# Windowed attention feeding a token and channel mixer on one core: more filler products in two places of the prologue, and a new order for three of the four hand-written period plans

## The chip, the cores and the metric

The kernel runs on one core of one Trainium2 chip. The metric is the device time of the whole program in microseconds (us). Lower is better. "Before" has a median of 307.49 us over 5 runs.

## What is computed

For each of 8 batches: 8 heads of attention over 576 positions with 64 dimensions, where a position sees the 32 positions on either side of it and 8 global positions (and the global positions see all and are seen by all). The attention output, laid out as 576 x 512, is the input x of a mixer block with four weights:

```
x = attention(q, k, v, global_idx)            # 576 x 512 per batch
u = x + (relu(x^T @ w_tok1) @ w_tok2)^T       # across tokens: 576 -> 256 -> 576
out = u + relu(u @ w_ch1) @ w_ch2             # across channels: 512 -> 1536 -> 512
```

Nearly all multiplications are in the last line.

## The kernel before, in words

**The work of a batch.** All products are in 16-bit floats with sums in PSUM. Positions are cut into 5 row tiles (four of 128, one of 64), heads into 4 pairs. The steps of one batch, with the letters that the plans use for them and their lines:

- T, Q, K (L434 to L454): T transposes one head pair of q and k on TensorE, Q and K copy the result from PSUM to the tiles qT and kT (VectorE unless told otherwise). R and r (L459, L470) do so for the last 64 positions. CQ and CK (L418) cast q and k to 16 bits ahead of T, on ScalarE. LP (L404) loads q and k for a whole batch. From batch 3 on another way is taken: Z (L393) loads q or k with a cast, issued by GpSimd's queue, into zq or zk, and Y (L399) transposes it into qT or kT with a DMA that SyncE's queue (SP) issues.
- S and X (L479, L500): the scores of one head pair in two halves, each a PSUM tile, and the exponential of a half on ScalarE into e_all. From batch 4 on, SS, XA and XB (L506, L529, L535) do two pairs at a time. M (L542) multiplies the band mask in on VectorE, with the columns of the global keys first (eg). VO (L409) makes a shifted copy of v on VectorE.
- GK, LX, LM (L578, L590, L597): scores of the global queries, exponential on ScalarE, mask on VectorE. OG and RF (L601, L612): the global positions' values on TensorE and their masking on VectorE. OG needs M of all four pairs.
- PV and NO (L717, L749): probabilities times values for one row tile on TensorE, division by the sum on VectorE. PV needs RF.
- A, RU, H, AD (L761 to L805): the two token products with a relu between them on ScalarE, and the sum u on VectorE.
- U (L835) transposes u into uT by DMA on SP's queue, two row tiles for each of U.0 and U.1, and U.2 the last rows. In period 0 TensorE does it instead (P and UT, L847 and L856).
- M4, M4l (L861, L872): the first channel product in 12 column blocks, 4 products of 128x512 each, with a relu on ScalarE; M4l are the last rows of two batches. All M4 of a batch need all of its uT. M5 (L886): the second channel product for one row tile in two parts of 6 products; after the second part VectorE adds u, and SP's queue sends the tile out.

**The order.** Nothing is scheduled by a tool: every engine runs its instructions in the order in which the program records them. After a prologue (L928 to L1075), which does the attention and token product of batch 0, there are 8 periods. Period b takes the dense units of batch b (M4, M4l, M5, in this order, one at each "D") and, between them, what `PLAN` says for other batches: a word that starts with n is for batch b+1, m for b+2, o for b+3, b for batch b itself. PLAN[0] and PLAN[1] serve periods 0 and 1. PLAN[2] serves periods 2, 4 and 6, PLAN[3] periods 3, 5 and 7 (L1085). A word is the step and its arguments; a last "v", "m", 0 or 1 names the PSUM place.

**PSUM.** There are four pools: two of one buffer for scores and others (0 and 1), one of one buffer (v), and psM with two buffers (m), which the M4 and M5 blocks use too. Two steps that use the same buffer wait for each other: the second score half of a pair waits for the exponential of the half that was in its buffer.

**The queues.** Loads with a cast (Z, LV, weights) are issued by GpSimd in program order; output and DMA transposes (Y, U) by SP in program order. A step behind a waiting one on such a queue waits with it.

**The fillers.** W(n) (L236) issues n products of the identity with itself, 128x512 each, whose result nobody reads. With `fresh` it takes a new psM buffer, otherwise one that was set aside. In the prologue there are W(2), W(5), W(3), W(3), W(1) and W(3, True).

The places that change in the prologue: L957, behind the first score half S_(0, 0, 0) and ahead of S_(0, 1, 0); and between OG0(3) (L1032) and RF0(3), where TensorE's next work is M1_0(1), the first token product of batch 0. OG0, RF0, PV0, NO0 and M1_0 (L620 to L685) are the forms by head pair that only batch 0 uses.

Of the kernel before, what the change touches and what calls it, by code (L numbers as in the profile page):

```python
# [25 lines left out]

PLAN = [
    """
    D D D nR.0 D nr nGL D nT.0.v nQ.0 nCK.2 D D nK.0 nCQ.2 D nT.1.v nK.1 nQ.1 nCQ.3 nCK.3 mLP D nS.0.0.0 mLV nS.0.1.1
    nX.0.1 nX.0.0 D nT.2.v nQ.2 nK.2 D nS.1.0.0 nX.1.0 nM.0 nS.1.1.1 nX.1.1 nT.3.v D nK.3 nM.1 nS.2.0.0 nS.2.1.1 nX.2.0  # L30
    nX.2.1 nQ.3 D nM.2 nVO nGK.v nLX nLM nS.3.0.0 nX.3.0 nS.3.1.1 nX.3.1 D nM.3 D nOG.v nRF nPV.0.v nPV.1.1 nNO.0 nNO.1
    D mCQ nPV.2.v nNO.2 nPV.3.1 D nNO.3 mCK mCQ.2 nA.0.0 mCQ.0 mCQ.3 nPV.4.1 nNO.4 mCK.0 mCK.1 mR.m mr nA.1.0 nA.2.0
    nA.3.0 nA.4.0 nRU mCK.3 mCK.2 D mGL D mCQ.1 nH.0.v nAD.0 nH.1.0 nAD.1 D nP.0 nUT.0 mT.0.m nP.1 mQ.0 mK.0 mT.1.m mK.1
    mS.0.0.0 nUT.1 mS.0.1.1 mX.0.0 mX.0.1 mT.2.m mQ.1 mQ.2 mK.2 mM.0
    """,
    """
    mZ.0.1 mZ.1.0 mZ.1.2 mZ.0.4 nT.3.v nS.1.0.0 nS.1.1.1 mZ.1.1 nX.1.0 mZ.1.3 nQ.3 D nX.1.1 nK.3 D mZ.0.3 mZ.0.0 mZ.1.4
    D nS.2.1.1 mZ.0.2 nX.2.1 nS.2.0.0 nX.2.0 nM.1 nVO D nGK.v nLX nM.2 nS.3.0.0 nX.3.0 nS.3.1.1 nLM nX.3.1 D nM.3 D
    nOG.0 nRF D D nPV.0.v.h nPV.1.1 nNO.0 mY.0.2 mY.0.3 bHL nPV.2.0 bAT bU.2 mY.0.1 nNO.1 D mY.1.2 nNO.2 mY.0.0 D D
    nA.0.1 nPV.3.v nNO.3 nPV.4.0 nNO.4 mY.1.1 D nA.1.1 nA.2.1 D nA.3.1 mY.1.4 nA.4.1 mY.1.0 mY.0.4 nRU D mLV mY.1.3 D  # L40
    mGL nH.0.0 nAD.0 D nU.0 nH.1.1 nAD.1 nU.1 D D bGC bGT.0 oZ.1.2 bGE mS.1.0.v mX.1.0 D mS.0.0.1 mS.0.1.0 oZ.0.2 oZ.1.0
    mX.0.0 oZ.1.1 oZ.0.4 oZ.0.1 oZ.0.3 oZ.0.0 mX.0.1 oZ.1.3 D mS.1.1.0 mX.1.1 mM.0 mS.2.0.1 mX.2.0 mS.2.1.v mM.1 mX.2.1
    D mS.3.1.1 mS.3.0.0 mX.3.0 oZ.1.4 mX.3.1 D mM.2 mVO mM.3 D D mOG.0 mGK.v mLX mLM mRF D
    """,
    """
    D nPV.0.v.h nNO.0 nPV.1.1 mY.0.0 nNO.1 nPV.2.0 nNO.2 mY.0.2 bAT mY.0.3 D D nA.0.1 mY.1.2 nA.1.1 mY.1.4 mY.0.4 D
    nA.2.1 mY.1.3 nPV.3.v mY.1.1 nPV.4.0 mY.0.1 mY.1.0 nNO.3 D D nA.3.1 nNO.4 nA.4.1 nRU D D mLV nH.0.0 D nAD.0 nU.0 mGL
    D D nH.1.0 nAD.1 oZ.0.1 oZ.0.0 D nU.1 oZ.0.2 D mSS.0 mXA.0 mXA.1 mXB.0 oZ.0.3 oZ.0.4 oZ.1.1 D mM.0 D oZ.1.4 mM.1
    oZ.1.0 D oZ.1.3 D oZ.1.2 mSS.1 mXA.2 mXA.3 mXB.1 mVO D mM.2 mM.3 D mGK.v mLX mOG.1 mRF mLM D
    """,  # L50
    """
    D bHL mY.1.0 nPV.1.1 nNO.1 nPV.2.0 nPV.0.v.h nNO.0 mY.0.0 mY.0.1 bAT nNO.2 mY.1.1 D mY.0.2 bU.2 D D nA.0.1 nPV.3.v
# [8 lines left out]
def kernel(  # L61
# [13 lines left out]
    B, H, S, D = q.shape  # L75
# [29 lines left out]
    def psm(shape, dtype=F32, name="m"):  # L105
        return psM.tile(shape, dtype, tag="m", name=name)
# [129 lines left out]
    def W(n, fresh=False):  # L236
        w = psm([P, 512], name="warm2") if fresh else warm
        for _ in range(n):
            nc.tensor.matmul(w.rearrange("p (a x) -> p a x", a=4), lhsT=ident, rhs=fill, start=True, stop=True)  # L239
# [230 lines left out]
    def TRE(b, tis=(0, 1), eng=nc.vector.tensor_copy):  # L470
        for ti in tis:
            v_ = st[b]["pr"][:, ti].rearrange("p i (n x) -> p n x i", n=NP)
            dst = qTs[b % 2][:, :, NT - 1, Q0 : Q0 + LAST] if ti == 0 else kTs[b % 2][:, :, WIN + 512 : WIN + S]
            eng(out=dst.rearrange("p n (x i) -> p n x i", i=4), in_=v_)
# [4 lines left out]
    def S_(b, p, part, at=None):  # L479
        qf = qTs[b % 2][:, p].rearrange("p t x -> p (t x)")  # L480
        kT = kTs[b % 2][:, p]
        ps = psx(at, [P, 2, 512], name=f"s{part}_{b}_{p}")
        a, z = ((0, 2 * QS), (2 * QS, ES))[part]
        if b == 0:
            for par in range(2):
                nc.tensor.matmul(ps[:, par, 0 : z - a], lhsT=ident, rhs=band[:, 0 : z - a], start=True, stop=False)
        js = ((0, 1, 2, 3, 4), (4, 5, 6, 7, 8, 9))[part]
        for j in js:
            i0 = max(qcol(j - 1), a)
            i1 = min(qcol(j) + HQ + Q0 * (j % 2 == 0), z)  # L490
            o = slice(HQ * (j % 2), HQ * (j % 2) + HQ)
            for par in range(2):
                r = slice(64 * par, 64 * par + 64)
                nc.tensor.matmul(  # L494
                    ps[o, par, i0 - a : i1 - a], lhsT=kT[r, HQ * j : HQ * j + HQ], rhs=qf[r, i0:i1],
                    start=b > 0, stop=b > 0 or j in js[-2:],
                )
        st[b]["s", p, part] = ps
# [121 lines left out]
    def OG0(p):  # L620
        s = st[0]
        if "rf" not in s:
            s["rf"] = mb.tile([P, NP, 2, VW], F16, tag="rf", name="rf_0")
        ps = psm([P, 2, VW], name=f"og0_{p}")
        s["og", p] = ps
        r = slice(32 * p, 32 * p + 32)
        for c in range(NT):
            nc.tensor.matmul(
                ps[r], lhsT=eg[:, c, 2 * p : 2 * p + 2, :], rhs=vsh[0][:, c, 2 * p : 2 * p + 2, :],
                start=(c == 0), stop=(c == NT - 1),  # L630
            )

    def RF0(p):
        s = st[0]
        r = slice(32 * p, 32 * p + 32)
        nc.vector.tensor_tensor(
            out=s["rf"][r, p], in0=s["og", p][r], in1=blk[r, 2 * p : 2 * p + 2].unsqueeze(2).to_broadcast([32, 2, VW]), op=ALU.mult
        )
# [23 lines left out]
    def NO0(p):  # L662
        pq = st[0]["pv", p][:, :, 0 : NT * VW].rearrange("p r (c x) -> p c r x", c=NT)
        rr = tiny.tile([P, NT, 2], F32, tag="rr0", name=f"rr0_{p}")
        nc.vector.reciprocal(out=rr, in_=pq[:, :, :, D])
        nc.vector.tensor_tensor(
            out=x16s[0][:, :, P * p : P * p + P].rearrange("p c (r x) -> p c r x", r=2), in0=pq[:, :, :, 0:D],
            in1=rr.unsqueeze(3).to_broadcast([P, NT, 2, D]), op=ALU.mult,
        )

    def M1_0(p):
        s = st[0]
        if "a1" not in s:
            s["a1"] = mb.tile([P, 2, DM], F16, tag="a1", bufs=1, name="a1_0")
            s["u16"] = mb.tile([P, 4, DM], F16, tag="u16", name="u16_0")
            s["ul"] = mb.tile([P, DM], F16, tag="ul", name="ul_0")
            s["uT"] = mb.tile([P, 4, 512], F16, tag="uT", name="uT_0")
        cols = slice(P * p, P * p + P)
        ps = psm([P, 2, P], name=f"a1p0_{p}")
        for tt in range(2):  # L680
            for ch in range(NT):
                w = w1[:, ch, P * tt : P * tt + P] if ch < NT - 1 else w1l[:, P * tt : P * tt + P]
                nc.tensor.matmul(ps[:, tt], lhsT=w, rhs=x16s[0][:, ch, cols], start=(ch == 0), stop=(ch == NT - 1))
        s["a1p", p] = ps
# [269 lines left out]
    S_(0, 0, 0)  # L954
    TRE(0, (0,), A)
    TRE(0, (1,), V)
    W(3)  # L957
    S_(0, 1, 0)
    SX(0, 0, 0)
    load_w1()  # L960
# [69 lines left out]
    PV0(0)  # L1030
    NO0(1)
    OG0(3)  # L1032
    RF0(3)
    M1_0(1)
    NO0(0)
# [86 lines left out]
```

## Time and profile before

| | us |
|---|---|
| median of 5 runs | 307.49 |
| lowest, highest | 306.23, 310.38 |
| the profiled execution | 310.13 |
| its span, from first to last instruction | 308.3 |

The profiled execution lies 2.64 us above the median, near the highest of the runs. Its granted TensorE clock is 1.00 throughout. TensorE is busy for 289.9 us of the span (94%), VectorE for 169.1, ScalarE for 135.5, GpSimd for 104.0. The 16 DMA engines moved 41.81 MB.

The stages of the span, cut where the first M4 of each batch starts:

| stage | from, to (us) | length | TensorE not busy |
|---|---|---|---|
| prologue | 0, 37.87 | 37.87 | 9.69 |
| period 0 | 37.87, 78.60 | 40.73 | 3.31 |
| period 1 | 78.60, 117.50 | 38.90 | 0.22 |
| period 2 | 117.50, 148.20 | 30.70 | 0.42 |
| period 3 | 148.20, 183.70 | 35.50 | 0.00 |
| period 4 | 183.70, 214.30 | 30.60 | 0.42 |
| period 5 | 214.30, 249.80 | 35.50 | 0.00 |
| period 6 | 249.80, 277.50 | 27.70 | 0.00 |
| period 7 | 277.50, 308.30 | 30.80 | 4.31 |

In rows of the timeline the columns are start, duration, engine (SPq is SyncE's queue), line, operation, tiles (written<-read), shape and count; in square brackets the idle time before the row and what ended it. A row's start is more certain than its end. In rows of waits they are the waiting engine and line, what ended the wait, the sum in us, the number of times and the longest.

### The profile page before, as it was taken

How to read it: one execution, taken by the hardware profiler on the slowest of the kernel's cores; microseconds unless marked ns; L12 is line 12 of the kernel's file. 1: busy time of each engine (PE TensorE's matmuls, PEld its weight loads, DVE VectorE, ACT ScalarE, POOL GpSimd, SP SyncE). 2: the span in 40 equal slices, each digit the busy share in tenths (PEclk: the TensorE clock that was granted, in tenths of full speed). 3: DMA queues.
4: the chain of work that ended last, by engine and by line, in shares of the span. 5: the costliest groups of instructions: out<-in, count | busy, mean ns of one | idle time of the engine just before them, and what ended most of it. 6: DMA issues, size and time to landing. Idle time of an engine off the chain costs nothing.

```text
span 308.3 us, 7871 instructions
## 1 busy us (share of the span) xinstructions
PE 289.9 (94%) x3310; PEld 157.6 (51%) x3310; DVE 169.1 (55%) x374; ACT 135.5 (44%) x225; POOL 104.0 (34%) x143
## 2 busy tenths in 40 slices
PE   4797899798999999999999999999999999999994
PEld 1356654455556445544556445444546455444643
DVE  7588557867973587238723756257613952321022
ACT  4570468533854153554345513634366415305500
POOL 6847657867002391057315720095000000000000
PEclk9999999999999999999999999999999999999999
DMA  6989999999906999979999998499954220231023
GB/s 190 218 152 195 297 206 133 289 196 175 112 3 100 100 178 216 119 108 146 208 147 128 121 214 134 85 138 198 187 79 80 102 70 2 51 119 53 0 83 89
DMA packets 138166, 41.81 MB, mean 136 GB/s; under 512 B 125779, under 2 KB 132371, under 8 KB 138131
## 3 DMA queue, kind: packets, MB, share of 16 engines
q0 software_dynamic: 85408, 18.75, 66.5%
q1 hardware_dynamic: 52720, 22.56, 38.5%
q8 instruction: 26, 0.43, 0.6%
q14 instruction: 10, 0.07, 0.1%
q10 hardware_dynamic: 2, 0.00, 0.0%
HBM read 36.04 MB, written 9.44 MB: 148 GB/s over the span
## 4 chain that ended last, share of the span: by engine, by line
PE 81%; DVE 8%; issue 5%; ACT 4%; DMA 1%; SPq 0%; DVEq 0%; ACTq 0%
PE b1p L867 26%; PE op L893 25%; PE a1p L769 5%; PE hp L792 4%; PE b1lp L880 3%; PE pv L726 3%; PE pv L735 3%; PE pT L438 2%; PE s L494 2%; PE warm L239 1%; DVE e_all L551 1%; DVE vod L411 1%; ACT e_all L504 1%; ACT e_all L537 1%; PE sa L522 1%
## 5 line engine op out<-in xcount | busy, mean ns | idle before, releaser
L870 ACT ACTIVATE b<-b1p 128x512 f16<-128x512 f32 x96 | 57.3, 600 | 82.3 <-PE b1p L867 82.2
L867 PE MATMUL b1p<-uT,wc 128*128 128x512 f16 x384 | 91.3, 379 | 0.0
L893 PE MATMUL op<-wc,b 128*128 128x512 f16 x372 | 85.1, 380 | 0.0
L867 PEld LDWEIGHTS <-wc 128*128 128x128 f16 x384 | 36.0, 98 | 41.4 <-issue 0.3
L893 PEld LDWEIGHTS <-b 128*128 128x128 f16 x372 | 34.7, 98 | 40.6
L897 DVE TENSOR_TENSOR osb<-u,op 128x512 f32<-128x512 f16 x31 | 21.2, 684 | 35.4 <-PE op L893 34.9
L395 POOL DMA_DIRECT2D zq<-in_q_dram x25 | 21.0, 853 | 54.7 <-DMA qT<-zq 52.5
L803 DVE TENSOR_TENSOR u<-x,hp 128x1024 f16<-128x1024 f16 x14 | 17.0, 1221 | 39.4 <-PE hp L792 39.4
L388 POOL DMA_DIRECT2D vsh<-in_v_dram x35 | 31.1, 895 | 10.5 <-DMA zq<-in_q_dram 3.2
L395 POOL DMA_DIRECT2D zk<-in_k_dram x25 | 21.1, 877 | 29.7 <-DMA kT<-zk 27.0
L504 ACT ACTIVATE e_all<-s 128x576 f16<-128x576 f32 (+1 forms) x32 | 21.8, 723 | 10.7 <-PE s L494 9.5
L551 DVE TENSOR_TENSOR e_all<-e_all,bandm 128x656 f16<-128x656 f16 x56 | 25.5, 497 | 1.0
L756 DVE TENSOR_TENSOR x<-pv,rr 128x512 f16<-128x512 f32 x35 | 24.2, 692 | 1.2
L531 ACT ACTIVATE e_all<-sa 128x864 f16<-128x864 f32 x16 | 13.6, 890 | 16.0 <-issue 13.8
L726 PE MATMUL pv<-rf,lf 128*64 128x264 f16 x140 | 18.2, 280 | 1.1 <-DVE rf L615 1.1
L735 PE MATMUL pv<-vsh,e_all 128*64 128x66 f16 x336 | 18.0, 194 | 0.0
L735 PEld LDWEIGHTS <-e_all 128*64 128x64 f16 x560 | 17.3, 111 | 0.0
L755 DVE RECIPROCAL rr<-pv 128x8 f32<-128x8 f32 x35 | 7.1, 203 | 17.9 <-PE pv L735 17.8
L769 PE MATMUL a1p<-x,w 128*128 128x512 f16 x56 | 15.4, 380 | 0.0
L792 PE MATMUL hp<-a,w 128*128 128x512 f16 x58 | 14.8, 379 | 0.0
L735 PE MATMUL pv<-vod,e_all 128*64 128x66 f16 x224 | 14.6, 194 | 0.0
L546 DVE TENSOR_TENSOR eg<-e_all,egm 128x80 f16<-128x80 f16 x28 | 5.5, 195 | 12.7 <-ACT e_all L537 10.9
(190 smaller groups left out, 347.5 us busy)
## 6 DMA issues: line engine op xcount, KB each, us to landing
out_dram<-osb SPq DMA_DIRECT2D x31, 256.0 KB
wc<-in_moe_w_ch_dram POOLq DMA_DIRECT2D x6, 512.0 KB
vsh<-in_v_dram POOLq DMA_DIRECT2D x21, 128.0 KB
zq<-in_q_dram POOLq DMA_DIRECT2D x20, 128.0 KB
zk<-in_k_dram POOLq DMA_DIRECT2D x20, 128.0 KB
lq<-in_q_dram POOLq DMA_DIRECT2D x2, 1024.0 KB
lk<-in_k_dram POOLq DMA_DIRECT2D x2, 1024.0 KB
vsh<-in_v_dram POOLq DMA_DIRECT2D x14, 96.0 KB
```

What stands on the lines that cost most here:

```text
L388: nc.gpsimd.dma_start(out=vsh[b % 2][r0:r1, c, :, 0:D], in_=v[b, :, j0 : j0 + (r1 - r0), :].rearrange("h p d -> p h d"),)
L395: nc.gpsimd.dma_start(out=(zq, zk)[ti][0:n, c], in_=(q, k)[ti][b, :, P * c : P * c + n, :].rearrange("h p d -> p h d"))
L504: nc.scalar.activation(out=e2[:, :, a:z], in_=ps[:, :, 0 : z - a], func=AF.Exp, scale=scale)
L551: nc.vector.tensor_mul(out=e2[:, par], in0=e2[:, par], in1=bm)
L726: nc.tensor.matmul(ps[r0 : r0 + 64, hf, 0 : NP * VW], lhsT=s["lf"][:, HQ * t : HQ * t + HQ], rhs=s["rf"][:, 2 * g : 2 * g + 2], start=True ...
L735: nc.tensor.matmul(ps[r0 : r0 + 64, hf, VW * hh : VW * hh + VW], lhsT=e_all[:, h, lo : lo + HQ], rhs=(vod if t % 2 else vsh)[b % 2][:, tau ...
L756: nc.vector.tensor_tensor(out=x16s[b % 2][r, tau, :].rearrange("p (f h x) -> p f h x", f=2, h=NP), in0=pq[r, :, :, 0:D], in1=rr[r].unsquee ...
L769: nc.tensor.matmul(ps[tt], lhsT=w, rhs=x16s[b % 2][:, ch, :], start=(ch == 0), stop=(ch == NT - 1))
L792: nc.tensor.matmul(ps[:, i, :], lhsT=w2[:, ch, P * tau : P * tau + P], rhs=s["a1"][:, ch, :], start=(ch == 0), stop=(ch == 1),)
L867: nc.tensor.matmul(ps, lhsT=wc1[:, cc, P * j : P * j + P], rhs=s["uT"][:, cc, :], start=(cc == 0), stop=(cc == 3))
L870: nc.scalar.activation(out=s["b1"][:, j, :], in_=ps, func=AF.Relu)
L893: nc.tensor.matmul(ps, lhsT=w, rhs=wc2[:, j, :], start=(j == 0), stop=(j == NJ - 1))
```

## The change

1. W(3) at L957 becomes W(5).
2. A W(4, True) is put in behind OG0(3), ahead of RF0(3) and M1_0(1).
3. PLAN[0], PLAN[1] and PLAN[2] are written in another order. PLAN[3] stays. The same steps are in them, with a few in another PSUM place. PLAN[2] is in force three times, in periods 2, 4 and 6.

The fillers, and the plans (old, then new; of PLAN[0] up to the token product, of the others the stretches that differ most):

```diff
@@ prologue
     TRE(0, (1,), V)
-    W(3)
+    W(5)
     S_(0, 1, 0)
...
     NO0(1)
     OG0(3)
+    W(4, True)
     RF0(3)
     M1_0(1)
@@ PLAN[0]
-    D D D nR.0 D nr nGL D nT.0.v nQ.0 nCK.2 D D nK.0 nCQ.2 D nT.1.v nK.1 nQ.1 nCQ.3 nCK.3 mLP D nS.0.0.0 mLV nS.0.1.1
-    nX.0.1 nX.0.0 D nT.2.v nQ.2 nK.2 D nS.1.0.0 nX.1.0 nM.0 nS.1.1.1 nX.1.1 nT.3.v D nK.3 nM.1 nS.2.0.0 nS.2.1.1 nX.2.0
-    nX.2.1 nQ.3 D nM.2 nVO nGK.v nLX nLM nS.3.0.0 nX.3.0 nS.3.1.1 nX.3.1 D nM.3 D nOG.v nRF nPV.0.v nPV.1.1 nNO.0 nNO.1
+    D D D nR.1 D nr nT.0.v D nCQ.2 D nGL nK.0 D nQ.0 D nS.0.0.0 nCK.2 nT.1.v nCQ.3 nS.0.1.1 nCK.3 mLP mLV nX.0.0 nK.1
+    nQ.1 nX.0.1 D D nT.2.v nQ.2 nK.2 nM.0 nS.1.0.0 nX.1.0 nS.1.1.1 D nX.1.1 nT.3.v nK.3 D nS.2.0.0 nS.2.1.1 nM.1 nX.2.0
+    D nQ.3 nX.2.1 nM.2 nVO nGK.v nLX nS.3.0.0 nX.3.0 nS.3.1.1 nLM nX.3.1 D nM.3 D nOG.0 nRF nPV.0.v nNO.0 nPV.1.1 nNO.1
...
-    nA.3.0 nA.4.0 nRU mCK.3 mCK.2 D mGL D mCQ.1 nH.0.v nAD.0 nH.1.0 nAD.1 D nP.0 nUT.0 mT.0.m nP.1 mQ.0 mK.0 mT.1.m mK.1
-    mS.0.0.0 nUT.1 mS.0.1.1 mX.0.0 mX.0.1 mT.2.m mQ.1 mQ.2 mK.2 mM.0
+    nA.3.0 nA.4.0 nRU D mCK.3 D nH.0.v nH.1.0 nAD.0 mCK.2 mCQ.1 nAD.1 D nP.0 mGL nUT.0 mT.0.m mT.1.m mQ.0 mK.0 mK.1 nP.1
+    mS.0.0.0 nUT.1 mX.0.0 mS.0.1.1 mX.0.1 mT.2.m mQ.1 mQ.2 mK.2 mM.0
@@ PLAN[1]
-    mZ.0.1 mZ.1.0 mZ.1.2 mZ.0.4 nT.3.v nS.1.0.0 nS.1.1.1 mZ.1.1 nX.1.0 mZ.1.3 nQ.3 D nX.1.1 nK.3 D mZ.0.3 mZ.0.0 mZ.1.4
-    D nS.2.1.1 mZ.0.2 nX.2.1 nS.2.0.0 nX.2.0 nM.1 nVO D nGK.v nLX nM.2 nS.3.0.0 nX.3.0 nS.3.1.1 nLM nX.3.1 D nM.3 D
+    mZ.1.0 nT.3.v nS.1.0.0 mZ.1.2 nX.1.0 mZ.0.1 mZ.0.4 nS.1.1.1 mZ.0.0 nX.1.1 D D nS.2.1.1 mZ.0.2 nX.2.1 nK.3 nS.2.0.0
+    nX.2.0 mZ.1.1 mZ.1.4 nM.1 mZ.1.3 nQ.3 D nVO D nGK.v mZ.0.3 nS.3.0.0 nX.3.0 nS.3.1.1 nM.2 nX.3.1 D nLX nM.3 nLM D
...
-    D mS.3.1.1 mS.3.0.0 mX.3.0 oZ.1.4 mX.3.1 D mM.2 mVO mM.3 D D mOG.0 mGK.v mLX mLM mRF D
+    mX.2.1 mS.3.1.1 mS.3.0.0 D mX.3.1 oZ.1.4 mVO mX.3.0 mM.2 mM.3 D D mOG.0 mGK.1 mLX mLM mRF D
@@ PLAN[2]
-    D nPV.0.v.h nNO.0 nPV.1.1 mY.0.0 nNO.1 nPV.2.0 nNO.2 mY.0.2 bAT mY.0.3 D D nA.0.1 mY.1.2 nA.1.1 mY.1.4 mY.0.4 D
-    nA.2.1 mY.1.3 nPV.3.v mY.1.1 nPV.4.0 mY.0.1 mY.1.0 nNO.3 D D nA.3.1 nNO.4 nA.4.1 nRU D D mLV nH.0.0 D nAD.0 nU.0 mGL
-    D D nH.1.0 nAD.1 oZ.0.1 oZ.0.0 D nU.1 oZ.0.2 D mSS.0 mXA.0 mXA.1 mXB.0 oZ.0.3 oZ.0.4 oZ.1.1 D mM.0 D oZ.1.4 mM.1
-    oZ.1.0 D oZ.1.3 D oZ.1.2 mSS.1 mXA.2 mXA.3 mXB.1 mVO D mM.2 mM.3 D mGK.v mLX mOG.1 mRF mLM D
+    mY.1.3 D nPV.1.1 nPV.0.v.h nNO.0 mY.0.0 nNO.1 nPV.2.0 mY.1.4 nNO.2 mY.0.2 mY.1.1 bAT mY.0.3 D D nA.0.1 nA.1.1 mY.0.4
+    D nA.2.1 nPV.3.v mY.0.1 nPV.4.0 mY.1.0 nNO.3 mY.1.2 D D nA.3.1 D nNO.4 nA.4.1 nRU mLV D D nH.0.0 mGL nAD.0 nU.0 D D
+    nH.1.v nAD.1 oZ.0.1 D D mSS.0 oZ.0.4 D D oZ.1.1 oZ.1.4 oZ.0.2 mXA.0 mXA.1 nU.1 oZ.0.0 mXB.0 oZ.0.3 mM.0 mM.1 oZ.1.0
+    oZ.1.3 oZ.1.2 D D mSS.1 mXA.2 mXA.3 mXB.1 mVO D mM.2 mM.3 D mGK.v mOG.1 mRF mLX mLM D
```

In the built program TensorE has 6 products more (3316 for 3310); the other engines have the same instructions in another order. On SP's queue the two transposes of U.1 stand, in periods 1, 2, 4 and 6, behind the batch's first output tile instead of ahead of it; most transposes of Y change places among themselves, and so do the loads of Z on GpSimd's queue.

## The prediction

> **What bounds the kernel now.** I read the page first, then TensorE's waits, then the timelines of the places that change. The page names TensorE as the bound, and its clock as fully granted, so only time in which TensorE waits can be won, and only what makes it wait can be lost.
>
> ```profile
> PE 289.9 (94%) x3310; PEld 157.6 (51%) x3310; DVE 169.1 (55%) x374; ACT 135.5 (44%) x225; POOL 104.0 (34%) x143
> ...
> PEclk9999999999999999999999999999999999999999
> ```
>
> By stage (the table above) TensorE idles 9.69 us in the prologue, 3.31 in period 0, 0.22 in period 1, 0.42 in each of periods 2 and 4, nothing in 3, 5 and 6. So new orders for periods 0, 1, 2, 4 and 6 fight over 3.31 + 0.22 + 0.84 = 4.4 us at most. The waits of the whole span, as TensorE's own list names them:
>
> ```profile
> PE og L606 <- DVE eg L546: 1.4, 3, 0.6
> ...
> PE pv L649 <- issue: 1.1, 1, 1.1
> PE pv L726 <- DVE rf L615: 1.1, 1, 1.1
> ...
> PE pu L854 <- DVE uT L859: 0.7, 1, 0.7
> PE s L494 <- ACT e_all L504: 0.6, 1, 0.6
> ```
>
> **Part 1: two fillers more at L957.** TensorE's timeline of the prologue:
>
> ```profile
> 12.81 1.46 PE L239 MATMUL warm<-ident 128*128 128x512 f16 x3
> 14.06 0.61 PE L486 MATMUL s<-band,ident 128*128 128x288 f16 x2
> 14.61 0.32 PE L494 MATMUL s<-qT,kT 64*64 64x80 f16 x10
> 14.86 0.82 PE L239 MATMUL warm<-ident 128*128 128x512 f16 x3
> 15.52 0.39 PE L438 MATMUL pT<-ident,qn 128*128 128x128 f16 x4
> ```
>
> Start to next start, the first three fillers take (14.06 - 12.81)/3 = 0.42 us each, the later three (15.52 - 14.86)/3 = 0.22: the array ran at half speed until about 14.3 us. Two more fillers cost 0.84 if both are slow, 0.43 if both are fast. The first would start at 14.06 (slow), the second at 14.48 (fast): 0.64. The two L486 products behind them would then be fast: 0.55 falls to about 0.34 (18.32 to 18.66 for the same shape), so the sum is 0.64 - 0.21 = +0.43. Nothing covers it: SX, T(0,2), its copies and the chain down to NO0(1) follow this row in TensorE's order. Possible cover comes later, at 31.1, where a product of PV0(2) waits 1.14 us for "issue" with no semaphore; if that ends at a fixed time, up to 1.14 us of delay vanishes in it. Bounds 0 and +0.84; I take +0.43.
>
> The Trainium skill ("TensorE: Matmul & The Clock Gate", "The HAM clock gate") says that the clock is halved by default and after an idle window of about 3.4 us, freed after as much sustained work, and that the window runs free of the program. By the rule, fillers might free the clock earlier in executions where the window falls badly, up to one window of half speed (some 1.7 us) saved. By the row, the clock was free at 14.3 with three fillers, and the two new ones start at 14.06, too late to bring that forward. I count +0.43 by the row and keep the rule's gain for a rival.
>
> **Part 2: W(4, True).**
>
> ```profile
> 27.08 0.46 PE L628 MATMUL og<-vsh,eg 128*32 128x132 f16 x5
> ...
> 28.44 0.38 PE L683 MATMUL a1p<-x,w 128*128 128x128 f16 x4 [0.89 <-DVE x L666]
> ```
>
> Four fast fillers are 0.88 us. Five products of 132 columns end their issue at about 27.36, so the fillers run until 28.24, and M1_0(1) can't start before 28.44, where VectorE's x lands. The row's idle time covers them: 0. They shift with part 1 as x does. The price without cover would be 0.88. The other risk is the buffer: if M1_0(1) had to take og0_3's, it would wait for RF0(3), whose VectorE row starts at 28.41 and takes 0.30: +0.27. In the built program it takes the fillers' own buffer and waits for the same VectorE step as before. As to the clock, the gap of 0.89 us is far below the rule's 3.4, and the products behind it are fast, so nothing is gained either. I take 0, bounds 0 and +0.27.
>
> **Part 3: period 0.** Here lies the money.
>
> ```profile
> 51.97 0.78 ACT L504 ACTIVATE e_all<-s 128x736 f16<-128x736 f32 x1 [0.86 <-PE b1p L867]
> ...
> 52.80 0.35 PE L494 MATMUL s<-qT,kT 64*64 64x80 f16 x12 [0.64 <-ACT e_all L504]
> ...
> 55.67 1.14 DVE L411 COPY vod<-vsh 64x2112 f16<-64x2112 f16 x1
> 56.84 0.96 DVE L412 COPY vod<-vsh 64x2112 f16<-64x2112 f16 x1
> ...
> 58.92 0.46 PE L606 MATMUL og<-vsh,eg 128*32 128x132 f16 x17 [0.60 <-DVE eg L546]
> ...
> 59.73 0.70 DVE L615 TENSOR_TENSOR rf<-og,blk 128x528 f16<-128x528 f32 x1
> ...
> 60.48 0.30 PE L726 MATMUL pv<-rf,lf 128*64 128x264 f16 x2 [1.10 <-DVE rf L615]
> ```
>
> S.2's second half waits for X.1.1, OG for M.3, PV for RF: 2.34 us. But they are one chain: from the end of X.1.1 (52.75) VectorE works without a pause through M.1, Q.3, M.2, VO, LM, an output sum and M.3 to RF's end at 60.43, 7.68 us. PV starts there whatever TensorE does. The new order keeps VectorE's sequence from M.1 to RF as it is, so PV moves by as much as M.1 does. The new order brings S.0 up by 1 to 2 M4 blocks and X.1.1 behind M4(10)'s relu. Adding up TensorE's rows (0.86 per M4, 0.44 per T, 0.09 at each change between full and partial tiles), T.2 starts at 48.7, S.1.1 ends at 49.65, M4(10) ends at 50.7, its relu runs 50.95 to 51.55, X.1.1 some 51.45 to 52.24. Masking follows at 52.3 instead of 52.78: about -0.45. The 0.86 of idle time ahead of X.1.1 is not in the order (TensorE's products were through at 50.3 by their rows), so it may be this execution's own; without it the old order would lose less, and the new one gain nothing. Bounds -1.2 and +0.3; -0.45. The period's end (P, T, Q, K, 74 to 78.6) hangs on VectorE's copies, in the same order as before: 0, though T.1 now fills a gap of 0.69.
>
> **Part 4: period 1.** The rows show S.3 held to 83.84 by X.2.0, 0.21 beyond its place, and OG by M.3 for 0.15 net. In the new order two M4 stand between S.2 and S.3, so X.2.0 (some 82.3 to 82.95) is done before S.3 (83.5), and M.3 before OG: -0.36 to -0.46 by the sums; -0.4, bounds -0.5 and +0.3.
>
> **Part 5: periods 2, 4, 6.** The number of changes between full and partial tiles (0.09 us each) is the same in both programs, and OG's wait (M.3 behind XB.1, 0.42) keeps its place. What moves is U.1. SP's queue in period 2:
>
> ```profile
> 134.40 5.18 SPq L842 DMA_TRANSPOSE uT<-u  x4
> 139.67 9.81 SPq L898 DMA_DIRECT2D out_dram<-osb  x4
> ```
>
> The four transposes of uT were issued from 134.40 to 139.58 and landed, by their semaphores, at 137.87, 141.75, 144.42 and 145.56; M4(0) of batch 3 starts at 148.23, so there were 2.67 us to spare (period 4: 210.37 against 214.29, 3.92). Now U.1 is queued behind the first output tile, whose VectorE sum ends at 139.13: it goes out at about 139.7 and 141.0, 2.7 later. If its own latency of 7.3 stays, it lands at 148.3: period 2 waits up to 0.3, period 4 none, and period 6 has no loads beside it. "DMA: Bandwidth & Descriptors", "Issuing engines are not separate DMA queues", speaks against the change: all queues share the 16 engines, so U.1 now shares them with that output and with Z and V loads that GpSimd issues from 134.77 to 149. By the rule, another 1 us for the 256 KB output at the 195 GB/s that the stretch 142 to 150 shows (1.3): 1.3 + 0.3 in period 2 and nothing in 4. By the row it is the same queue with the same sum of work, whose fifth transfer landed at 147.21: 0. Bounds 0 and +2; +0.3.
>
> **The sum.** +0.43 + 0 - 0.45 - 0.4 + 0.3 = -0.12 us. On the profiled 310.13 that is 310.0; the median stands 2.64 below it, and I take the difference over: 307.4.
>
> **The rivals.** (a) Slower: uT comes late. With 2.67 spare in period 2 and 3.92 in period 4, landing decides once it is over 148.2 and 214.3; at 4 us later than before it costs 1.3 + 0.1, at 5.5 later 2.8 + 1.6 and 1 in period 6: between +1.4 and +5, 308.9 to 312. For: a queue at its fullest in exactly these stretches. Against: SP's queue carries no more than before. (b) Faster: the clock or period 0 gives more than the profiled execution tells. Half of one slow window in the prologue (0.85) or part 3 at its bound (1.2), with part 4 and no cost of part 1 and 5: -1.6 to -2, some 305.5. For: runs spread from 306.23 to 310.38, so some stage varies. Against: PV can't pass VectorE. (c) The fillers are the whole effect: both slow, the plans neutral: +0.84 + 0.27 = +1.1, 308.6. For: each is on TensorE's chain; against: the 1.14 us wait at 31.1 behind them.
>
> **How the numbers follow.** That gains and losses cancel within 1 us: 0.57, at 307.4. (a) 0.18, (b) 0.12, (c) 0.13. One per cent is 3.07 us, about what a measurement of this kernel can tell from no change; only the far parts of (a) and (b) pass it: slower 0.14, faster 0.06, within 0.80. The range reaches to the far side of (b), -0.4 of part 4 on top of -1.7 (305.4), and up to the bounds of parts 1, 2 and 5 together, +0.84 + 0.27 + 2 (310.6).
>
> **What would show it.** Right: five L239 products ahead of the second L486 row and everything behind later by about 0.4 until 31; M1_0(1) still released by x; PV of period 0 still released by RF, some 0.45 earlier than its stage's start would give; no wait ahead of OG in period 1; M4(0) of batches 3, 5 and 7 without a gap. Wrong: a gap ahead of those M4(0); L867 or L438 rows at 0.42 per 512 columns behind 15 us in one kernel alone; M1_0(1) waiting for RF0(3).

## The result and the profile after

| | before | changed |
|---|---|---|
| median (us) | 309.09 of 79 runs | 310.98 of 42 runs |
| lowest, highest | 305.30, 314.35 | 308.28, 314.69 |
| profiled execution, its span | 310.13, 308.3 | 312.9, 311.1 |

The ratio changed to before is 1.0085, with a 95% interval of 1.0066 to 1.0103: 2.0 to 3.2 us slower. Ratios here leave out executions more than 1.5% above their kernel's fastest, which also hides part of what a steadier clock wins, so where the fillers are the subject I give medians and counts over all executions. By the medians the loss is 1.9 us. The forecast was 307.4, in a range up to 310.6. Of the miss of 3.6 us, 1.6 is the base, whose median rose from 307.49 to 309.09 with more runs; the other 2.0 is the change, forecast at -0.1.

The page of the changed kernel says that TensorE is still the bound, but on the chain that ended last DMA has grown from 1% to 9%, and SP's queue from 0% to 5%. The chain before:

```profile
PE 81%; DVE 8%; issue 5%; ACT 4%; DMA 1%; SPq 0%; DVEq 0%; ACTq 0%
```

The page of the changed kernel, with its chain as the last line:

```profile
PE 291.6 (94%) x3316; PEld 157.7 (51%) x3316; DVE 168.2 (54%) x374; ACT 135.1 (43%) x225; POOL 103.7 (33%) x143
...
PEclk9799999999999999999999999999999999999999
DMA  6989999999909999399999997599943220141023
...
PE 75%; DMA 9%; DVE 5%; SPq 5%; ACT 3%; issue 1%; DVEq 0%
```

TensorE's list of waits (engine, line, what ended the wait, sum, times, longest) has a new first row. In the kernel before uT was in no row for L867.

```profile
PE b1p L867 <- DMA uT<-u: 2.9, 2, 1.7
...
PE og L606 <- DVE eg L546: 1.2, 3, 0.4
PE pv L726 <- DVE rf L615: 1.1, 1, 1.1
PE s L494 <- ACT e_all L504: 0.9, 1, 0.9
...
PE sa L522 <- DMA kT<-zk: 0.4, 1, 0.4
...
PE a1p L683 <- DVE x L666: 0.2, 1, 0.2
```

TensorE's timeline shows the two places: the first M4 of batch 3 and of batch 5, at the ends of periods 2 and 4.

```profile
149.59 1.04 PE L867 MATMUL b1p<-uT,wc 128*128 128x512 f16 x4 [1.68 <-DMA uT<-u]
...
217.06 1.04 PE L867 MATMUL b1p<-uT,wc 128*128 128x512 f16 x4 [1.22 <-DMA uT<-u]
```

Stage by stage (cut at the first M4 of each batch), changed minus before: prologue -0.93, period 0 +0.37, period 1 -0.56, period 2 +2.48, period 3 0, period 4 +1.40, periods 5 to 7 0. The sum is the 2.8 us between the spans. The first two vary by more than this from one execution to the next and period 1 by up to 0.35; the others repeat within 0.1 us unless something waits. For the kernel before this takes the starts of M4 from the rows: that of batch 1 is at 79.13, not at 78.60 as in the table of stages, so that period 0 takes 41.26 and period 1 38.38.

SP's queue in period 2 (start, duration of the issues, count) shows what happened to U.1.

```profile
133.56 2.51 SPq L842 DMA_TRANSPOSE uT<-u  x2
138.68 0.35 SPq L898 DMA_DIRECT2D out_dram<-osb  x1
139.08 3.50 SPq L842 DMA_TRANSPOSE uT<-u  x2
142.68 6.32 SPq L898 DMA_DIRECT2D out_dram<-osb  x3
```

U.1 goes out behind the first output tile, and its two issues take 3.50 us where U.0's take 2.51. By the completion events in the trace the two land at 148.15 and 149.55: 9.1 and 8.3 us after their issues. M4(0) starts at 149.59, with the last of them.

In period 4 U.1 moves further. The queue before, then in the changed kernel:

```profile
199.31 5.24 SPq L842 DMA_TRANSPOSE uT<-u  x4
205.22 10.32 SPq L898 DMA_DIRECT2D out_dram<-osb  x4
```

```profile
206.60 0.35 SPq L898 DMA_DIRECT2D out_dram<-osb  x1
207.01 3.55 SPq L842 DMA_TRANSPOSE uT<-u  x2
```

Counted from the period's start, U.1's last issue goes from 19.6 to 24.3 us.

### The profile page after: what moved, and what is told of

It reads as the page before. It is cut to its first block, busy times and chain, and to the rows that moved or that the text cites. A ratio compares the mean times of both kernels' runs of the same rounds, so it can differ in the third digit from the quotient of the medians.

```text
span 311.1 us, 7884 instructions
## 1 busy us (share of the span) xinstructions
PE 291.6 (94%) x3316; PEld 157.7 (51%) x3316; DVE 168.2 (54%) x374; ACT 135.1 (43%) x225; POOL 103.7 (33%) x143
## 4 chain that ended last, share of the span: by engine, by line
PE 75%; DMA 9%; DVE 5%; SPq 5%; ACT 3%; issue 1%; DVEq 0%
PE b1p L867 24%; PE op L893 23%; DMA uT<-u 5%; PE a1p L769 5%; PE hp L792 3%; PE b1lp L880 3%; PE pv L726 3%; PE pv L735 3%; SPq L402 2%; DMA lkr<-in_k_dram 2%; PE s L494 1%; SPq L842 1%; PE warm L239 1%; DMA kT<-zk 1%; PE pT L438 1%
## 5 line engine op out<-in xcount | busy, mean ns | idle before, releaser
L867 PE MATMUL b1p<-uT,wc 128*128 128x512 f16 x384 | 91.7, 379 | 3.0 <-DMA uT<-u 2.9
L867 PEld LDWEIGHTS <-wc 128*128 128x128 f16 x384 | 35.9, 98 | 45.4 <-DMA uT<-u 3.9
L388 POOL DMA_DIRECT2D vsh<-in_v_dram x35 | 30.7, 897 | 5.9 <-DMA lk<-in_k_dram 2.1
L504 ACT ACTIVATE e_all<-s 128x576 f16<-128x576 f32 (+1 forms) x32 | 21.5, 720 | 10.6 <-PE s L494 10.2
L531 ACT ACTIVATE e_all<-sa 128x864 f16<-128x864 f32 x16 | 13.6, 890 | 16.6 <-issue 13.8
L769 PE MATMUL a1p<-x,w 128*128 128x512 f16 x56 | 15.4, 380 | 0.0
L735 PE MATMUL pv<-vod,e_all 128*64 128x66 f16 x224 | 14.7, 194 | 0.0
L792 PE MATMUL hp<-a,w 128*128 128x512 f16 x58 | 14.6, 379 | 0.0
```

Source lines behind the costliest of these rows:

```text
L388: nc.gpsimd.dma_start(out=vsh[b % 2][r0:r1, c, :, 0:D], in_=v[b, :, j0 : j0 + (r1 - r0), :].rearrange("h p d -> p h d"),)
L504: nc.scalar.activation(out=e2[:, :, a:z], in_=ps[:, :, 0 : z - a], func=AF.Exp, scale=scale)
L735: nc.tensor.matmul(ps[r0 : r0 + 64, hf, VW * hh : VW * hh + VW], lhsT=e_all[:, h, lo : lo + HQ], rhs=(vod if t % 2 else vsh)[b % 2][:, tau ...
L769: nc.tensor.matmul(ps[tt], lhsT=w, rhs=x16s[b % 2][:, ch, :], start=(ch == 0), stop=(ch == NT - 1))
L792: nc.tensor.matmul(ps[:, i, :], lhsT=w2[:, ch, P * tau : P * tau + P], rhs=s["a1"][:, ch, :], start=(ch == 0), stop=(ch == 1),)
L867: nc.tensor.matmul(ps, lhsT=wc1[:, cc, P * j : P * j + P], rhs=s["uT"][:, cc, :], start=(cc == 0), stop=(cc == 3))
```

## The experiments

Theory A: the late U.1 of PLAN[2] (periods 2 and 4) is the whole loss. Theories B and C of the first four runs: the new order of loads and Y transposes, or the fillers and the clock. Each "over" or "under" is against the kernel before, run on the same chip.

**1. U.1 late, alone.**

```diff
-    ... D nU.1 oZ.0.2 D mSS.0 ... oZ.1.1 D mM.0 D oZ.1.4
+    ... D oZ.0.2 D mSS.0 ... oZ.1.1 D mM.0 nU.1 D oZ.1.4
```

> The kernel before, with nothing changed but the place of U.1 in PLAN[2]: behind M5(0,1), so that its two transposes stand behind the first output tile on SP's queue. Theory A (the place of U.1 in the queue is what costs): M4(0) of batch 3 waits 1 to 2 us for uT and that of batch 5 about 1 us, so the time is 2 to 3.5 us over the kernel before (ratio 1.007 to 1.011). Theory B (the new order of Z, Y and V loads crowds the transposes, U.1's place alone is harmless because the queue carries the same sum): 0 to +0.3 us, no wait ahead of M4(0). Theory C (fillers and clock): 0.

Ratio 1.0047 (1.0020 to 1.0075): 1.45 us over. Less than A asked, more than B and C. In the profile uT lands 0.27 us ahead of need in period 2, and period 4 is 0.43 longer; the rest of the 1.45 this one profile doesn't show.

**2. The changed kernel with U.1 early.**

```diff
-    nH.1.v nAD.1 oZ.0.1 D D mSS.0 ... mXA.0 mXA.1 nU.1 oZ.0.0
+    nH.1.v nAD.1 nU.1 oZ.0.1 D D mSS.0 ... mXA.0 mXA.1 oZ.0.0
```

> The changed kernel with U.1 of PLAN[2] moved back to right behind AD.1, ahead of the first output tile; all else as changed. Theory A: no wait ahead of M4(0) of batches 3 and 5; what remains is the gain of the prologue and of period 1, so 0 to 1.5 us under the kernel before (ratio 0.995 to 1.000). Theory B: uT still comes late, +2 to +3 us (1.007 to 1.010). Theory C: +1 us or more, without a wait ahead of M4(0).

Ratio 0.9972 (0.9942 to 1.0002), no wait ahead of any M4(0), periods 2 and 4 at 30.72 us as before. One word's place takes back 3.5 us (1.0085 less 0.9972, of 309). C falls, and B alone too, since all the new loads are still there.

**3. The whole new PLAN[2] alone** (its text is in the diff above).

> The kernel before with the whole new PLAN[2] and nothing else of the change. Theory A: as with U.1 alone moved, 2 to 3.5 us over the kernel before, and about the full loss of the change plus 0.5 to 1, since what it wins elsewhere is not in it. Theory B: also +2 to +3.5; it differs from A only by what U.1 alone gives. Theory C: within 0.3 us of the kernel before.

Ratio 1.0100 (1.0064 to 1.0136): 3.1 us over. Between this and run 1 stands something else in PLAN[2] that hurts only when U.1 is late. The profile has periods 2 and 4 longer by 1.88 and 1.30.

**4. The fillers alone** (both edits).

> The kernel before with the two edits of fillers alone (W(5) for W(3), and the new W(4, True)). Theory A: between -1 and +0.5 us: the two cold fillers cost up to 0.84, and the 1.14 us in which a product of PV0(2) waits for no semaphore, together with the gap ahead of M1_0(1), takes it back, or the stall is gone as in the profile of the changed kernel. Theory C (fillers and clock make the loss): +1.5 to +3 us.

Ratio 1.0001 (0.9976 to 1.0027); medians of all executions 308.11 against 308.73. This is A; the loss that C asked for isn't there.

**5. PLAN[0] alone.**

> The kernel before with the new PLAN[0] alone. Theory A (the VectorE chain of period 0 starts 0.45 us earlier, as predicted): 0.3 to 0.6 us under the kernel before. Theory B (the exponential X.1.1 is late by about a microsecond wherever it stands, and the new order puts more behind it): PV of period 0 starts 23 us or more after the period's start, where the kernel before shows 22.6, and the time is 0.3 to 1.2 us over the kernel before.

Ratio 1.0032 (1.0002 to 1.0063), 1.0 us over, but the medians of all executions are 307.82 and 307.31 with wide spread, and its profile has PV 21.6 us after the period's start: neither theory's picture. The gain of A isn't there; more is said below.

**6. PLAN[1] alone.**

> The kernel before with the new PLAN[1] alone. Theory A (S.3 and OG no longer wait in period 1, as predicted): period 1 takes 37.8 to 38.0 us instead of 38.4, the time is 0.3 to 0.6 us under the kernel before. Theory B (the period's new order of Y and Z, or U.1 of period 1 behind the first output tile, gives it back at the start of period 2): a wait ahead of M4(0) of period 2 and a time within 0.3 us of the kernel before or over it.

Period 1 takes 37.75 us in the profile (38.37 to 38.67 in all nine profiled kernels with the old PLAN[1]), and M4(0) of period 2 has no wait. The ratio, 0.9997 (0.9963 to 1.0031), can't resolve 0.5 us in its 14 runs: A by the profile, not by the time.

**7. New PLAN[2] with U.1 late, but with later loads.**

```diff
-    D nA.2.1 nPV.3.v mY.0.1 nPV.4.0 mY.1.0 nNO.3 mY.1.2 D D nA.3.1
+    D nA.2.1 nPV.3.v nPV.4.0 mY.1.0 nNO.3 mY.1.2 mY.0.1 D D nA.3.1
```

> The kernel before with the new PLAN[2], U.1 behind the first output tile, and one word more moved: Y.0.1 goes last of the batch's Y, so that the first Z load, which must wait for it, and with it the row of Z and V loads on GpSimd's queue starts about 2.6 us later than in the new PLAN[2]. Theory A (the early Z and V loads are what makes a late U.1 land so late): the loss falls from the 3.1 us of the new PLAN[2] to that of U.1 alone or under it, 0 to +1.5 us over the kernel before; U.1's last transpose lands 6 to 7 us after its issue. Theory B (the loads don't matter; the place on SP's queue alone costs, and the two earlier runs differ by chance): +2 to +3 us, latency still 8 us or more.

Ratio 1.0016 (0.9983 to 1.0049): of the 3.1 us most is gone, as A said. But only period 2 lost its wait, and there 1.2 of the 1.9 us by which uT lands earlier than in run 3 are an earlier issue; from issue to landing it still took 7.3. Period 4 is 1.13 us longer than before and its last transpose took 8.4 us to land, which is B's latency.

**8. U.1 late as in run 1, with earlier loads.**

```diff
-    D nA.2.1 mY.1.3 nPV.3.v mY.1.1 nPV.4.0 mY.0.1 mY.1.0
+    D nA.2.1 mY.0.1 nPV.3.v mY.1.3 nPV.4.0 mY.1.1 mY.1.0
```

> The kernel before with U.1 late as in the first experiment and, beside it, only the three transposes Y.0.1, Y.1.3 and Y.1.1 in another order, so that the first Z load finds its place free two transposes (2.6 us) earlier. Theory A (late U.1 and early loads together make the loss): 2 to 3.5 us over the kernel before, M4(0) of batch 3 waits 1 to 2.5 us, the last uT lands 8 us or more after its issue. Theory B (U.1's place alone): as in the first experiment, 0.5 to 1.5 us over, latency under 7 us.

Ratio 1.0202 (1.0147 to 1.0256), from 6 executions: 6.2 us over, more than either theory. TensorE's waits show a second victim that I hadn't thought of, the last transpose of K, for which SS.0 waits:

```profile
PE sa L522 <- DMA kT<-zk: 2.8, 2, 2.2
PE b1p L867 <- DMA uT<-u: 2.1, 2, 1.4
```

So here the transposes of Y that are still on their way land later, and through SS.0 they hold up the output tile and U.1 behind it: U.1's last issue comes 3.2 and 1.0 us later than in run 1, and it lands 7.6 us after it in both periods, not the 8 or more of A. That the early Z loads are the cause is argued, since the order of the Y transposes changed with them. This run mixes two waits and proves less than it was meant to.

**9 to 12. What is in flight beside U.1.** The changed kernel, each time with fewer bytes and the same instructions. `h` heads of 8 for Z (and in the same way for V), `w` columns of 512 for the output tile. The other heads of batches 5 to 7 are not loaded and the other columns not written, so these kernels only test the transfers:

```diff
+        h = H if b < 5 else 1
-            out=(zq, zk)[ti][0:n, c], in_=(q, k)[ti][b, :, P * c : ...
+            out=(zq, zk)[ti][0:n, c, 0:h], in_=(q, k)[ti][b, 0:h, P * c : ...
...
+                w = DM if tau or b not in (2, 4) else 64
-                nc.sync.dma_start(out=out[b, P * tau : P * tau + P, :], in_=osb)
+                nc.sync.dma_start(out=out[b, P * tau : P * tau + P, 0:w], in_=osb[:, 0:w])
```

Z cut:

> The changed kernel, but the Z loads of batches 5 to 7 (those issued in periods 2 to 4) move one head of eight: the rest of q and k of these batches isn't loaded, so that the attention of these batches is computed on stale data. Same instructions on every engine. Theory A (what is in flight beside U.1 delays it, and Z is most of it): U.1 lands within 6 us of its issue, no wait or under 0.3 us ahead of M4(0) of batches 3 and 5, the time is 0 to 1.5 us under the kernel before. Theory B (U.1's later issue alone): still 2 to 3 us over. Theory C (the output tile ahead of it on the queue): still 2 to 3 us over.

V cut:

> The changed kernel, but the V loads of batches 5 to 7 move one head of eight (the other seven keep the values of an earlier batch). Theory A with Z as the load that matters: 1 to 3 us over the kernel before, a little less than the changed kernel. Theory A with V as the load that matters (V's packets are in flight when U.1 lands): 0 to 1.5 us under the kernel before, no wait ahead of M4(0). Theories B and C: 2 to 3 us over.

Output tile cut:

> The changed kernel, but the first output tile of batches 2 and 4, the transfer ahead of U.1 on SP's queue, writes 64 columns of 512 (the rest of these two tiles is left unwritten). Theory C (U.1 waits for the 256 KB ahead of it): U.1 lands 1.3 us or more earlier, the time is at most 1 us over the kernel before. Theories A and B: 2 to 3 us over, U.1 lands as late as in the changed kernel within 0.5 us.

Z and V cut:

> The changed kernel with both the Z and the V loads of batches 5 to 7 cut to one head of eight (stale data in their place). Theory A: U.1 lands 3 to 5 us after its issue, no wait ahead of M4(0), 0.3 to 1.7 us under the kernel before. Theory B: 2 to 3 us over. Theory C: 1.5 to 3 us over.

Ratios: Z cut 1.0009 (0.9978 to 1.0039), V cut 1.0025 (0.9992 to 1.0057), output tile cut 1.0053 (1.0002 to 1.0104), both loads cut 0.9975 (0.9940 to 1.0011). Against the changed kernel's 1.0085 (1.0066 to 1.0103) each cut of a load takes something back, and both loads together take all of it; the output tile's cut isn't clear of it by the time. The profiles say how. Times after the start of period 2 / period 4, from SP's and GpSimd's issues and the completion events; M4(0) is due at 30.72:

| kernel | first Z load | last U.1 issued | last uT landed | from issue to landing | period longer by |
|---|---|---|---|---|---|
| before | 17.3 / 16.2 | 20.8 / 19.6 | 28.1 / 26.8 | 7.3 / 7.2 | 0 / 0 |
| 1, U.1 late | 17.0 / 16.7 | 23.6 / 23.7 | 30.5 / 31.1 | 6.8 / 7.4 | 0 / 0.43 |
| 2, changed, U.1 early | 15.4 / 14.8 | 20.2 / 19.8 | 28.1 / 28.1 | 7.9 / 8.4 | 0 / 0 |
| 3, new PLAN[2] | 16.2 / 14.9 | 24.6 / 24.3 | 32.5 / 32.0 | 7.9 / 7.6 | 1.88 / 1.30 |
| changed | 16.3 / 14.7 | 24.8 / 24.3 | 33.2 / 32.1 | 8.3 / 7.8 | 2.48 / 1.40 |
| 7, loads late | 18.4 / 18.1 | 23.4 / 23.4 | 30.7 / 31.8 | 7.3 / 8.4 | 0 / 1.13 |
| 8, loads early | 14.6 / 13.5 | 26.9 / 24.6 | 34.5 / 32.3 | 7.6 / 7.6 | 3.79 / 1.60 |
| 9, Z cut | 16.6 / 14.8 | 23.8 / 23.4 | 29.5 / 30.3 | 5.7 / 6.9 | 0.43 / 0 |
| 10, V cut | 16.2 / 15.1 | 24.1 / 24.0 | 32.0 / 30.7 | 7.9 / 6.6 | 1.37 / 0 |
| 11, output tile cut | 15.9 / 14.8 | 23.8 / 24.3 | 30.8 / 31.6 | 7.0 / 7.3 | 0.15 / 0.90 |
| 12, Z and V cut | 16.8 / 14.8 | 23.9 / 23.3 | 26.8 / 25.8 | 2.9 / 2.5 | 0.58 / 0 |

Wherever the last uT lands after 30.7, the period is longer by about the difference. The 0.43 and 0.58 of runs 9 and 12 come with SS.0's wait for the last Y, which the new order has beside (0.21 and 0.37 of idle time there, 0.42 in the changed kernel; the rest no row names). The output tile's cut brings the landing 2.3 us forward in period 2, as C asked, and 0.5 in period 4, as A asked. Of the 2.3, 1.0 is U.1's earlier issue, in an execution without SS.0's wait.

With the loads cut U.1 lands 2.9 and 2.5 us after its last issue; in the kernel before it took 7.3 and 7.2. Period 6, where no loads run, shows the same without any cut: there the changed kernel's U.1 stands behind the same output tile,

```profile
273.27 0.35 SPq L898 DMA_DIRECT2D out_dram<-osb  x1
273.67 2.53 SPq L842 DMA_TRANSPOSE uT<-u  x2
```

and lands 2.5 us after its last issue, as in the kernel before, where it stands ahead of the tile. The stretch from the first output tile's issue to the landing, in the changed kernel and in run 12 (columns: length; busy time of PE, PEld, DVE, ACT, POOL; clock; DMA share; GB/s):

```profile
138.60:149.60 11.00, 8.90 (x110) 4.10 (x108) 9.05 (x20) 3.30 (x6) 6.92 (x8) 1.00 2.07 165
```

```profile
136.30:141.00 4.70, 4.70 (x64) 2.31 (x63) 4.15 (x10) 1.18 (x3) 2.61 (x5) 1.00 0.94 181
```

The packets' own time adds up to 2.07 times what 16 engines have with the loads, and to 0.94 times with the loads cut: U.1's packets are in flight among many others.

**13. W(4, True) alone.**

> The kernel before with the new W(4, True) behind OG0(3) alone. Theory A (in part of the executions the clock is halved in a stretch that begins in the idle time ahead of M1_0(1), and these four fillers prevent it): the share of executions with a mean granted clock under 0.99 falls from about 0.5 to under 0.2, and the time is 0.5 to 1.5 us under the kernel before. Theory B (these fillers change nothing, as predicted): share as before, time within 0.3 us of it.

Medians of all executions 306.33 against 307.31, and A's count: a mean clock under 0.99 in 1 of 22, against 35 of 75 before on the same chip. The ratio, 1.0010 (0.9985 to 1.0036), shows none of this, for the reason given with the result. Over all runs of this study the count is 16 of 218 in the kernels with W(4, True), 59 of 125 in the others, 121 of 251 in the kernel before. Under 0.985, as low as the profiles below, it is 0 of 218 and 65 of 251.

**14. W(5) alone.**

> The kernel before with W(5) for W(3) alone. Theory A (the other fillers keep the clock; these two only cost): the share of executions with a mean clock under 0.99 stays at about 0.5, the time is 0.3 to 0.8 us over the kernel before. Theory B (these two keep the clock): the share falls under 0.2, and the time is 0 to 1 us under the kernel before.

10 of 22 under 0.99, ratio 1.0034 (1.0003 to 1.0066), medians 307.86 and 307.31: they don't keep the clock, and they cost, A.

**15. W(4, True) and the new PLAN[1].**

> The kernel before with only the two parts of the change that seem to gain: W(4, True) and the new PLAN[1]. Theory A (they add up): 1.3 to 2 us under the median of the kernel before over all its executions, share of executions with a clock under 0.99 below 0.15, and 4 to 5 us under the changed kernel. Theory B (one of them is chance): 0.3 to 1 us under.

Medians 306.97 against 308.09, 1.1 us under: between the theories, no more than W(4, True) alone gave. 0 of 22 under 0.99. Ratio 0.9981 (0.9958 to 1.0003).

**16. The same with W(1) at L957.**

> As the kernel with W(4, True) and the new PLAN[1], but W(1) in place of W(3) at L957. Theory A (the fillers at L957 only cost): another 0.3 to 0.8 us less than with W(3), share of low clocks unchanged. Theory B (some of them are needed to free or keep the clock): the clock comes free later or falls, and the time is the same or up to 1.5 us more than with W(3).

Medians 306.86 against 308.09, ratio 0.9972 (0.9947 to 0.9997). It is under the kernel before, but not clearly under run 15 (306.97). So two fillers less bring no 0.3 us that I could measure. By medians runs 13, 15 and 16 are under both kernels; the last is the one whose ratio says so too.

## Why the prediction was wrong, by its steps

**Part 5 failed, and it is more than the whole loss** (3.9 us in the profiles, of which the other parts win some back). The step that failed is the time of U.1's issue. The prediction had U.1 "2.7 later", worked out in period 2, and used the same for period 4 ("period 4 none"). Measured, its last issue moved by 4.0 us in period 2 and by 4.7 in period 4. Two things are in that.

- The place alone, run 1: 2.9 and 4.1 us later. In period 2 that is what was worked out. In period 4 the rows of the kernel before would have given more: U.1 was issued by 19.6 after the period's start, and the output tile that it now follows stands at 21.6. With 2.67 and 3.92 us to spare the place alone used up all there was.
- The rest of the new PLAN[2], which the prediction took at nothing ("the same queue with the same sum of work"): another 1.2 and 0.6 us. In period 2 the tile goes out 0.6 later than in run 1, behind SS.0's wait, and in both periods the first of the two issues takes 2.1 to 2.2 us where it took 1.2 before and 1.5 to 1.6 in run 1.

That U.1's "own latency of 7.3 stays" was nearly right: 8.3 and 7.8 us in the changed kernel, 1.1 and 0.6 more. In the eight profiles with the old PLAN[2] it is 6.6 to 7.9 and 7.1 to 7.7, in run 2, early in the new order, 7.9 and 8.4, and in run 1, late in the old order, 6.8 and 7.4. So the later place isn't what lengthens it; what else is in flight is, from 2.5 with no loads. Together uT lands 5.1 us later than before in period 2 and 5.3 in period 4; with 2.67 and 3.92 to spare that is 2.4 and 1.3, and the periods grew by 2.48 and 1.40.

Rival (a) had this wait and this formula ("at 5.5 later 2.8 + 1.6"), with 0.18 of the chance; only its "1 in period 6" didn't come, where no loads run. The rule of the Trainium skill ("DMA: Bandwidth & Descriptors", "Issuing engines are not separate DMA queues") spoke for it. Runs 9, 10 and 12 agree with the rule: what GpSimd's queue has in flight moves the landing of SP's transposes. Its price for the way to landing, 1.3 us, was not far from the 1.1 and 0.6 measured; the rest of the late issue stood in neither sum.

How the new order of Y and Z lengthens the issues and the way to landing isn't settled. Later loads brought uT forward by 1.9 us in period 2 (run 7 against run 3) and by 0.2 in period 4, where the last issue was 1.0 earlier and the way to landing 0.8 longer.

**Part 2 failed in sign.** I read the clock as fully granted from one execution and said "nothing is gained either". In about half of the executions of the kernel before it isn't so (run 13's counts). Nor is it so in the profiled execution: part 1 reads half speed from its rows until about 14.3 us, where the clock row says 1.00, so the clock row and the mean leave out this first slow stretch. The profile of run 1, which has no W(4, True), fell into such an execution: first TensorE's rows around M1_0(1), then the three stretches from 22.1.

```profile
23.50 0.46 PE L628 MATMUL og<-vsh,eg 128*32 128x132 f16 x5
25.55 0.58 PE L683 MATMUL a1p<-x,w 128*128 128x128 f16 x4 [1.59 <-DVE x L666]
```

```profile
22.10:25.60 3.50, 1.91 (x50) 1.59 (x50) 2.70 (x10) 0.00 (x0) 3.06 (x5) 1.00 1.05 156
25.60:29.00 3.40, 3.40 (x50) 2.98 (x50) 1.92 (x5) 0.38 (x1) 3.40 (x6) 0.50 1.20 226
29.00:32.40 3.40, 3.40 (x52) 2.98 (x50) 1.77 (x4) 0.38 (x1) 3.30 (x7) 0.50 1.00 301
```

TensorE idles for 1.59 us behind og's products, and from there its clock is 0.50 until 35.8. The profiles of runs 7 and 8 have the same 10 us of half speed from 25 on, with gaps of 1.24 and 1.05; none of the ten profiled kernels with W(4, True) has. The gap's length alone doesn't decide: in run 14, without these fillers, TensorE idles for 1.33 us at the same place and the clock stays at 1.00.

```profile
26.98 0.38 PE L683 MATMUL a1p<-x,w 128*128 128x128 f16 x4 [1.33 <-DVE x L666]
```

What else must come together stays open. With W(4, True), the same place in run 13:

```profile
25.70 1.04 PE L239 MATMUL warm<-ident 128*128 128x512 f16 x4
26.80 0.38 PE L683 MATMUL a1p<-x,w 128*128 128x128 f16 x4
```

The sizes fit: over all 251 runs of the kernel before, those with a clock under 0.99 have a median of 309.49, the others 306.93. Lowering their share from 35 of 75 to 1 of 22 is worth an estimated 0.42 x 2.56 = 1.1 us; run 13 measured 1.0. The profiles place the slow stretch only for means of 0.981 to 0.983; where executions between 0.985 and 0.99 lose theirs isn't shown. That the products ran free of cost was right (M1_0(1) is still released by x, after 0.20).

**Part 1** held in the profiled execution. The timeline of the changed kernel has five slow products, at 0.42 each, ahead of the second L486 row:

```profile
12.61 2.32 PE L239 MATMUL warm<-ident 128*128 128x512 f16 x5
14.72 0.47 PE L486 MATMUL s<-band,ident 128*128 128x288 f16 x2
```

That is the bound of +0.84, less what the rows behind them win. But whether the fillers here are slow belongs to the execution. In the profile of run 14 the clock is already full and five take 1.09 us, 0.22 each; it is full there in runs 2, 4 and 16 too.

```profile
11.14 1.25 PE L239 MATMUL warm<-ident 128*128 128x512 f16 x5
12.23 0.41 PE L486 MATMUL s<-band,ident 128*128 128x288 f16 x2
```

Run 14 has +0.55 by medians for the predicted +0.43, closer than its scatter allows to read. The 1.14 us inside PV0(2) that I had as possible cover is in none of the other profiles: it belonged to that execution.

**Part 3** gave nothing of its -0.45. The doubt that stood beside it was the point: the idle time ahead of X.1.1 "may be this execution's own". It belongs to a time and not to a word of the plan. In ten of the eighteen profiles ScalarE has such a gap, of 0.4 to 1.7 us, and the row behind it starts between 49.7 and 52.2 us, whichever it is: X.1.1 in the kernel before, another exponential in runs 1, 3, 4, 6, 8, 15 and 16 with the same PLAN[0]. In the changed kernel it is a relu:

```profile
51.21 0.60 ACT L870 ACTIVATE b<-b1p 128x512 f16<-128x512 f32 x1 [1.19 <-PE pT L438]
```

Counted from the period's start, PV comes at 21.5 to 24.5 us with the old PLAN[0] and at 21.6 to 23.9 with the new; in the eight profiles without the gap at 21.5 to 21.9 and 21.6 to 22.1. So the new order brings PV nothing. What makes the gap is open. "PV can't pass VectorE" held in every one: PV waits 1.10 for RF. Run 5's time leans to a loss of up to 2 us; why is open.

**Part 4** was right: period 1 takes 37.6 to 37.95 us with the new PLAN[1], 38.4 and more with the old; forecast -0.4, shown -0.5 by the profiles.

By medians of all executions the steps give -0.6 (fillers), +0.5 (PLAN[0]), -0.2 (PLAN[1]) and +2.4 (PLAN[2]), together +2.1 for the measured +1.9. That they meet so well is in part luck: by the ratios they give 4.0 us for 2.6, each known to about 1 us.

## What to carry to other kernels

Before a transfer is moved on its queue, work out its new time of issue in every place where the order is in force: here 2.9 us later in one period and 4.1 in the other, against 2.67 and 3.92 to spare. A transfer's latency in a trace belongs to what is in flight, not to the transfer: the same one took 2.5 us alone and 7 to 8 beside the loads. A dependent transfer goes ahead of the bulk transfers that nobody waits for, even on its own queue. One profiled execution says nothing of a clock that changes between executions: look at the clock of every run, and try to keep TensorE fed through gaps of 1 to 2 us if half of the runs lose time there.

## What the runs showed of the hardware

- Behind a gap of 1.59 us, in a stretch of 3.5 us in which TensorE was busy for 1.91, the clock was halved (run 1), and it stayed at half for 10.2 us though TensorE was busy throughout. Behind a gap of 1.33 us it wasn't (run 14), behind one of 1.05 it was (run 8). With four products in the gap no execution of 218 has a mean clock under 0.985, as these two have; of the kernel before 65 of 251 do. I had argued from a rule of the Trainium skill ("TensorE: Matmul & The Clock Gate", "The HAM clock gate": idle or busy windows of about 3.4 us) that so short a gap is harmless. Half-speed stretches of 3.41 us (11.4 to 14.8 in the changed kernel) and of three times that length do agree with its window. That section has the clock freed after at least one busy window; here it took three.
- The same two transposes took 2.5 to 2.9 us from last issue to landing with few or no loads beside them (DMA share 0.94 in run 12's period 2), and 7.2 to 8.3 beside the loads in the kernel before and the changed one (share 2.07 in the latter's period 2). Their issues on SP took 1.2 to 1.3 us each without loads and up to 2.5 with them (run 8).
- An issue on SP can be long without an output tile ahead of it: four issues of uT took 5.18 us in the kernel before and 6.25 in run 15, with the same order of U.
